# Reading two DRAM bounces in parts, and reordering the first batches, in a spectral-filter and channel-mix kernel

## The chip, the cores and the metric

The kernel runs on one core of a Trainium2 chip. The metric is the device time of one execution in microseconds (us). The kernel before takes 669.4 us (median of four runs, 668.0 to 670.7).

Names: PE is the matrix engine, ACT the scalar engine, DVE the vector engine, POOL the general engine, SP the sync engine, which here only issues DMAs. A line such as L344 is a line of the kernel's source; the same statement has another number in another version.

## The reference, cut to what matters

```python
def _attn_ref(x, w_r, w_i, b_r, b_i):            # x: 8 batches, 3072 positions, 256 channels
    X = np.fft.rfft(x, axis=1)
    Yr = Xr @ w_r - Xi @ w_i + b_r               # complex 256x256 product per frequency
    Yi = Xr @ w_i + Xi @ w_r + b_i
    ... soft threshold with lam = 0.01 ...
    return np.fft.irfft(Y, n=x.shape[1], axis=1)

def _moe_ref(x, mu_k, mu_r, w_k, w_v, w_r):      # x: the result of the above
    x_prev = ... x shifted by one position ...
    k = np.maximum((mu_k * x + (1 - mu_k) * x_prev) @ w_k, 0.0)
    v = k * k @ w_v
    return sigmoid((mu_r * x + (1 - mu_r) * x_prev) @ w_r) * v
```

## The kernel before

The transform of 3072 = 96 x 32 positions is done in two stages with matrix products, and the way back likewise. For each batch b there are three groups of work on PE:

- first(b): 16 products of 512 columns, giving A (96 partitions, by quarters q of the 32 indices n2);
- middle(b): second transform, complex mix, threshold, and second transform back, giving V;
- last(b): first transform back, giving YT, from which the token products (L575, L600, L617) of the batch are made.

Between first and middle, and between middle and last, the data changes its partition axis. This is done by a bounce through DRAM: A goes out to Adr and comes back as A2, V goes out to Vdr and comes back as V2. The two bounces are what the change touches:

```python
# first(b), after the quarter q has been copied out of PSUM
nc.sync.dma_start(out=Adr[b][:, 8 * q:8 * q + 8, :], in_=a)
if q == 3:
    at(k + WRITE_US, fetch)
def fetch(k):                                     # four DMAs, each to 32 partitions, 512-byte runs
    A2[b] = a2_pool.tile([128, NG, D], BF16, name="A2")
    for cj in range(4):
        nc.sync.dma_start(out=A2[b][32 * cj:32 * cj + 32],
                          in_=Adr[b][24 * cj:24 * cj + 24].rearrange("g n d -> n g d"))
    done["A2", b] = k + READ_US                   # what the planner believes
# middle(b), after the unit u (of six) has been copied out of PSUM
for cj in range(4):                               # four stores a unit, 512-byte runs
    nc.sync.dma_start(out=Vdr[b][24*cj + 4*u:24*cj + 4*u + 4].rearrange("g n d -> n g d"),
                      in_=vt[32 * cj:32 * cj + 32])
def fetch(k):                                     # after the sixth: four DMAs to 96 partitions, 4 KB runs
    for q in (2, 3, 0, 1):
        nc.sync.dma_start(out=V2[b, q], in_=Vdr[b][:, 8 * q:8 * q + 8, :])
    done["V2", b] = k + READ_US
```

The order of the instructions on every engine is fixed while the kernel is built, by a planner in Python. It keeps a clock of its own and takes, whenever PE is free by that clock, the unit with the earliest due time whose needs are `done`. Each engine and the SP queue then run that order: at one L501 of the changed kernel PE stood 18.8 us with 16 products behind it (L629) that do not read what it waited for.

```python
READ_US, WRITE_US = 7.0, 5.0
...
fb += first(b, 0.0, 1.0) if b == 0 else first(b, *((45.0, 52.0) if b == 1 else (s - 0.9 * P, s - 0.1 * P)))
fa += middle(b, 20.0, 44.0) if b == 0 else middle(b, s, s + 0.5 * P)
fc += last(b, 55.0, 60.0) if b == 0 else last(b, s + 0.75 * P, s + 0.95 * P)
```

Of the kernel before, what the change touches and what calls it, by code (L numbers as in the profile page):

```python
# [22 lines left out]
def kernel(  # L23
# [31 lines left out]
        return ctx.enter_context(tc.tile_pool(name=name, bufs=bufs))  # L55

    a_pool, a2_pool, xt_pool, xt0_pool = pool("ap", 3), pool("a2p", 2), pool("xtp", 3), pool("xt0p", 1)
    r1_pool, ym_pool, v_pool, v2_pool = pool("r1p", 2), pool("ymp", 3), pool("vp", 3), pool("v2p", 4)
    yt_pool, mx_pool, rl_pool, k2_pool = pool("ytp", 2), pool("mxp", 2), pool("rlp", 3), pool("k2p", 2)
    rg_pool, o_pool = pool("rgp", 3), pool("op", 2)  # L60

# [147 lines left out]


    heap, seq = [], itertools.count()
    free = {"pe": 0.0, "act": 8.0, "dve": 14.0}
    done, slots = {}, {}

    def at(key, fn):
        heapq.heappush(heap, (key, next(seq), fn))
# [53 lines left out]


    Adr, A2, Vdr, V2, YT = {}, {}, {}, {}, {}
    READ_US, WRITE_US = 7.0, 5.0

    def first(b, t0, t1):

        live = {}

        def make(q, p):
            def issue(ps, h, end):  # L280
                if p == 0:
                    if q == 0:
                        Adr[b] = dram.tile([2 * 48, N2, D], BF16, name="Adr")
                    live["A"] = a_pool.tile([96, 8, D], BF16, name="A")
                xt, a = xs[b, q], live["A"]
                for i in range(2):
                    nc.tensor.matmul(ps[:96, 512 * i:512 * i + 512], FT,  # L287
                                     xt[:, 4 * p + 2 * i:4 * p + 2 * i + 2, :], start=True, stop=True)

                def evac(k):  # L290
                    e = copy(k, a[:, 4 * p:4 * p + 4, :], ps[:96].rearrange("p (n d) -> p n d", n=4),
                             1.03, 1.22)
                    release(h, e)
                    if p == 1:
                        at(e, store)

                def store(k):
                    nc.sync.dma_start(out=Adr[b][:, 8 * q:8 * q + 8, :], in_=a)
                    done["a", b, q] = k + WRITE_US
                    n = 4 * b + q + 4  # L300
                    if 8 <= n < 4 * B:
                        load_x(n // 4, n % 4)
                        done["x", n // 4, n % 4] = k + 9.0
                    if q == 3:
                        at(k + WRITE_US, fetch)

                def fetch(k):
                    A2[b] = a2_pool.tile([128, NG, D], BF16, name="A2")
                    for cj in range(4):
                        nc.sync.dma_start(out=A2[b][32 * cj:32 * cj + 32],  # L310
                                          in_=Adr[b][24 * cj:24 * cj + 24].rearrange("g n d -> n g d"))
                    done["A2", b] = k + READ_US
                    if b == 0:

                        nc.gpsimd.tensor_copy(out=junk, in_=A2[0][:, 0, 0:1])
                        load_big()
                        for n in range(4):
                            load_x(1, n)
                            done["x", 1, n] = k + 18.0

                at(end, evac)

            needs = [("x", b, q), "FT"] + [("mid", 0)] * (b == 1)
            if q == 3 and p == 1 and b >= 2:
                needs.append(("mid", b - 2))
            if q == 0 and p == 0 and b >= 2:
                needs.append(("A2", b - 2))
            n = 4 * b + q - 3
            if p == 0 and n >= 0:
                needs.append(("a", n // 4, n % 4))  # L330
            return Unit(t0 + (t1 - t0) * (2 * q + p) / 8, 0.44, needs, issue)

        return [make(q, p) for q in range(4) for p in range(2)]
# [3 lines left out]
    def middle(b, t0, t1):  # L337
# [76 lines left out]
        def back(u):  # L414
            def issue(ps, h, end):
# [2 lines left out]
                    nc.tensor.matmul(ps[:, 256 * i:256 * i + 256], GI[:, 4 * u + i, :],  # L418
                                     y[:, 256 * i:256 * i + 256], start=True, stop=True)
                if u == 0:  # L420
                    Vdr[b] = dram.tile([2 * 48, N2, D], BF16, name="Vdr")
                vt = v_pool.tile([128, 4, D], BF16, name="V")

                def evac(k):
# [2 lines left out]
                    at(e, store)  # L427

                def store(k):
                    for cj in range(4):  # L430
                        nc.sync.dma_start(
                            out=Vdr[b][24 * cj + 4 * u:24 * cj + 4 * u + 4].rearrange("g n d -> n g d"),
                            in_=vt[32 * cj:32 * cj + 32])
                    done["v", b, u] = k + WRITE_US
                    if u == NU - 1:
                        at(k + WRITE_US, fetch)

                def fetch(k):
                    for q in range(4):
                        V2[b, q] = v2_pool.tile([96, 8, D], BF16, name="V2")  # L440
                    for q in (2, 3, 0, 1):
                        nc.sync.dma_start(out=V2[b, q], in_=Vdr[b][:, 8 * q:8 * q + 8, :])
                    done["V2", b] = k + READ_US

                if u == NU - 1:
                    done["mid", b] = end
# [4 lines left out]
        for s in range(NU + 2):  # L451
# [10 lines left out]
            if 0 <= s - 2 < NU:  # L462
                u = s - 2
                needs = [("y", b, u), "GI"]
                if u == NU - 1 and b >= 1:
                    needs.append(("last", b - 1))
                n = 6 * b + u - 3
                if n >= 0:
                    needs.append(("v", n // 6, n % 6))
                units.append(Unit(f + 3 * g, 0.44, needs, back(u)))  # L470
# [4 lines left out]
    def last(b, t0, t1):  # L475
# [3 lines left out]
        def make(n, half, qd):  # L479
            def issue(ps, h, end):  # L480
# [5 lines left out]
                for i in range(4):  # L486
                    n2 = 16 * half + 4 * i + qd
                    for c in range(NCD):
                        nc.tensor.matmul(pv[:, c, :, i, :], V2[b, n2 // 8][:, n2 % 8, 128 * c:128 * c + 128],  # L489
                                         FI, start=True, stop=True)  # L490
                flat = yt.rearrange("p c h z n s -> p (c h) z n s")[:, :, half]

# [157 lines left out]
    def table_gi(n):  # L650
# [17 lines left out]
            at(end, evac)  # L668
        return issue

    def tables(k):
        make_g()
        run_on("act", k, 3.0)
        done["G"] = run_on("dve", free["act"], 0.5)

    P = 74.0
    START = 60.0
    tok, val, fa, fb, fc = [], [], [], [], []
    for b in range(B):
        s = START + P * (b - 1)  # L680
        fb += first(b, 0.0, 1.0) if b == 0 else first(b, *((45.0, 52.0) if b == 1 else (s - 0.9 * P, s - 0.1 * P)))
        fa += middle(b, 20.0, 44.0) if b == 0 else middle(b, s, s + 0.5 * P)
        fc += last(b, 55.0, 60.0) if b == 0 else last(b, s + 0.75 * P, s + 0.95 * P)
    for t in range(NT):
        s = START + P * t / 6
        d = P / 6
# [11 lines left out]
                            [("k2", t, i) for i in range(4)] + [("rg", t)], v_unit(t, p), part=p))  # L698

    for q in range(4):  # L700
        done["x", 0, q] = 5.0 + 3.3 * q
    done["FT"] = 8.0
    at(13.3, tables)
    tab = [Unit(18.0, 0.1, ["FT"], table_fi)]
    tab += [Unit(18.0 + n, 0.5, ["G"], table_gi(n)) for n in range(3)]
    streams = [tok, val, fa, fb, fc, tab]
    at(60.0 - 7.0, lambda k: mix_tokens(0, k))

    place, held, t = [0] * len(streams), {}, 0.0
    while any(n < len(s) for n, s in zip(place, streams)):  # L710
# [52 lines left out]
```

## Time and profile before

| | before |
|---|---|
| time, median | 669.4 us |
| span of the profiled run | 662.8 us |
| PE busy | 593.6 us (90%) |
| first L344 (middle(0) begins) | 31.97 us |
| first token product (L575) | 87.29 us |
| from there to the end | 575.5 us |

PE bounds the kernel from about 100 us on; the start is bound by the two bounces of batch 0, one after the other. The prediction below shows the lines for this. One more view is needed, the windows of the trace while A2 of batch 0 was read and nothing else ran. Columns: stretch, length, busy time of PE, weight loads, DVE, ACT and POOL with the number of instructions, granted PE clock, mean busy share of the 16 DMA engines, GB/s.

```profile
26.00:28.00 2.00, 0.00 (x0) 0.00 (x0) 0.00 (x0) 0.00 (x0) 0.00 (x0) 0.50 1.20 193
28.00:30.00 2.00, 0.00 (x0) 0.00 (x0) 0.00 (x0) 0.00 (x0) 0.00 (x0) 0.50 1.20 177
```

A DMA to 32 partitions in runs of 512 bytes moved about 185 GB/s, with a busy share of 1.20 for the 16 engines (above 1, so it serves here only for comparison).

### The profile page before, as it was taken

How to read it: one execution, taken by the hardware profiler on the slowest of the kernel's cores; microseconds unless marked ns; L12 is line 12 of the kernel's file. 1: busy time of each engine (PE TensorE's matmuls, PEld its weight loads, DVE VectorE, ACT ScalarE, POOL GpSimd, SP SyncE). 2: the span in 40 equal slices, each digit the busy share in tenths (PEclk: the TensorE clock that was granted, in tenths of full speed). 3: DMA queues.
4: the chain of work that ended last, by engine and by line, in shares of the span. 5: the costliest groups of instructions: out<-in, count | busy, mean ns of one | idle time of the engine just before them, and what ended most of it. 6: DMA issues, size and time to landing. Idle time of an engine off the chain costs nothing.

```text
span 662.8 us, 12033 instructions
## 1 busy us (share of the span) xinstructions
PE 593.6 (90%) x4722; PEld 435.5 (66%) x4801; DVE 483.8 (73%) x732; ACT 443.5 (67%) x469; POOL 25.2 (4%) x57
## 2 busy tenths in 40 slices
PE   4295379999999989998999989999999999999996
PEld 1273247777776767765777767766777777777764
DVE  5164368788778877797678787688677896788883
ACT  6254357767777767776577767778687767766662
POOL 5021000000000000000000000000000000000000
PEclk9689579999999999999999999999999999999999
DMA  8697996362247954488155874379233852362223
GB/s 182 119 189 166 290 213 121 79 183 65 57 112 175 230 128 111 103 227 197 33 128 128 237 146 96 88 202 207 86 104 104 223 113 68 78 183 56 65 72 88
DMA packets 75593, 90.33 MB, mean 136 GB/s; under 512 B 8976, under 2 KB 59920, under 8 KB 75536
## 3 DMA queue, kind: packets, MB, share of 16 engines
q1 hardware_dynamic: 69696, 75.53, 44.5%
q0 software_dynamic: 5840, 14.03, 12.5%
q8 instruction: 37, 0.61, 0.4%
q14 instruction: 20, 0.16, 0.1%
HBM read 53.22 MB, written 50.33 MB: 156 GB/s over the span
## 4 chain that ended last, share of the span: by engine, by line
PE 66%; DMA 17%; ACT 6%; DVE 5%; issue 3%; SPq 1%; POOL 0%; DVEq 0%; ACTq 0%; POOLq 0%
PE banks L617 22%; PE banks L575 19%; PE banks L394 11%; DMA Adr<-A 7%; DMA A<-Adr 6%; PE banks L600 4%; ACT rl L581 3%; PE banks L361 3%; PE banks L418 2%; PE banks L383 2%; ACT A L234 2%; PE banks L287 2%; DMA Vdr<-V 1%; DVE V L236 1%; PE banks L489 1%
## 5 line engine op out<-in xcount | busy, mean ns | idle before, releaser
L581 ACT ACTIVATE rl<-banks 128x1024 bf16<-128x1024 f32 x192 | 195.0, 1029 | 86.1 <-PE banks L575 73.2
L575 PE MATMUL banks<-xk,wk 128*128 128x512 bf16 x706 | 191.1, 383 | 4.0 <-DVE xk L553 1.4
L617 PE MATMUL banks<-wv,k 128*128 128x256 bf16 x1536 | 184.5, 274 | 0.4 <-DVE k L587 0.3
L587 DVE TENSOR_TENSOR k<-rl 128x1024 bf16<-128x1024 bf16 x192 | 131.8, 687 | 53.6 <-ACT rl L581 53.5
L617 PEld LDWEIGHTS <-k 128*128 128x128 bf16 x1536 | 150.3, 98 | 30.1 <-issue 1.8
L575 PEld LDWEIGHTS <-wk 128*128 128x128 bf16 x768 | 73.4, 98 | 57.9 <-issue 4.3
L394 PEld LDWEIGHTS <-XT 128*128 128x128 bf16 x768 | 75.4, 98 | 23.9 <-issue 0.8
L402 ACT ACTIVATE r<-banks,neglam 128x1024 bf16<-128x1024 f32 x48 | 53.4, 1113 | 40.6 <-PE banks L394 39.4
L406 DVE SCALAR_TENSOR_TENSOR Y<-banks,r 128x1024 bf16<-128x1024 f32 x48 | 58.5, 1222 | 28.1 <-ACT r L402 28.0
L394 PE MATMUL banks<-wr,XT 128*128 128x256 bf16 x384 | 73.8, 274 | 0.9
L394 PE MATMUL banks<-wi,XT 128*128 128x256 bf16 x384 | 73.8, 274 | 0.0
L553 DVE SCALAR_TENSOR_TENSOR xk<-diff,muk,YT 128x512 bf16<-128x512 bf16 x96 | 70.0, 746 | 0.6
L553 DVE SCALAR_TENSOR_TENSOR xr<-diff,mur,YT 128x512 bf16<-128x512 bf16 x96 | 69.2, 745 | 0.0
L624 DVE TENSOR_TENSOR o<-banks,rg 128x1024 f32<-128x1024 f32 x48 | 58.5, 1218 | 7.7 <-PE banks L617 7.7
L234 ACT ACTIVATE XT<-banks 128x1024 bf16<-128x1024 f32 (+2 forms) x39 | 37.8, 970 | 35.4 <-PE banks L361 23.5
L234 ACT ACTIVATE A<-banks 96x1024 bf16<-96x1024 f32 x49 | 49.2, 1020 | 17.6 <-DMA Adr<-A 12.0
L287 PE MATMUL banks<-xs,FT 96*96 96x512 bf16 x128 | 39.5, 420 | 19.0 <-ACT A L234 11.7
L600 PE MATMUL banks<-wrm,xr 128*128 128x256 bf16 x384 | 49.8, 272 | 3.5 <-ACT rl L581 2.2
L234 ACT ACTIVATE YT<-banks 128x768 bf16<-128x768 f32 x51 | 39.9, 815 | 16.2 <-PE banks L489 16.2
L605 ACT ACTIVATE rg<-banks 128x1024 bf16<-128x1024 f32 x48 | 49.2, 1026 | 1.9 <-PE banks L600 1.9
L600 PEld LDWEIGHTS <-xr 128*128 128x128 bf16 x384 | 37.1, 97 | 14.1 <-issue 3.8
L234 ACT ACTIVATE V<-banks 128x1024 bf16<-128x1024 f32 x33 | 33.8, 1023 | 9.9 <-PE banks L418 8.1
(91 smaller groups left out, 401.8 us busy)
## 6 DMA issues: line engine op xcount, KB each, us to landing
out_dram<-o SPq DMA_DIRECT2D x192, 128.0 KB, 2.2
xs<-in_x_dram POOLq DMA_DIRECT2D x32, 384.0 KB, 8.1
Adr<-A SPq DMA_DIRECT2D x32, 384.0 KB, 6.6
A<-Adr SPq DMA_DIRECT2D x32, 384.0 KB, 6.6
Vdr<-V SPq DMA_DIRECT2D x192, 64.0 KB, 1.8
V<-Vdr SPq DMA_DIRECT2D x32, 384.0 KB, 6.2
wk<-in_moe_w_k_dram POOLq DMA_DIRECT2D x1, 512.0 KB, 5.4
wv<-in_moe_w_v_dram POOLq DMA_DIRECT2D x1, 512.0 KB, 8.4
```

Of the source, the lines that this page charges most:

```text
L234: nc.scalar.activation(out, in_, AF.Copy, bias=0.0, scale=1.0)
L287: nc.tensor.matmul(ps[:96, 512 * i:512 * i + 512], FT, xt[:, 4 * p + 2 * i:4 * p + 2 * i + 2, :], start=True, stop=True)
L394: nc.tensor.matmul(o, lhs, w[:, c, :], start=False, stop=(w is wi and c == NCD - 1 and (i == 1 or not (u or half))))
L402: nc.scalar.activation(r1, ps, AF.Relu, bias=neglam, scale=1.0)
L406: nc.vector.scalar_tensor_tensor(out=y, in0=ps, scalar=LAM, in1=r1, op0=ALU.add, op1=ALU.min)
L553: nc.vector.scalar_tensor_tensor(out=m[:, c, :], in0=df[:, c, :], scalar=mu[:, c:c + 1], in1=yp[:, c, :], op0=ALU.mult, op1=ALU.add)
L575: nc.tensor.matmul(ps[:, 512 * f:512 * f + 512], wk[:, c, 128 * ff:128 * ff + 128], xk[:, c, :], start=(c == 0), stop=(c == NCD - 1))
L581: nc.scalar.activation(rl, ps, AF.Relu, bias=0.0, scale=1.0)
L587: nc.vector.tensor_tensor(out=k2, in0=rl, in1=rl, op=ALU.mult)
L600: nc.tensor.matmul(ps[:, 256 * q:256 * q + 256], xr[:, c, 128 * q:128 * q + 128], wrm[:, c, :], start=(c == 0), stop=(c == NCD - 1))
L617: nc.tensor.matmul(ps[:, 256 * q:256 * q + 256], K2[t][:, ff, 128 * q:128 * q + 128], wv[:, ff, :], start=(ff == 0), stop=(ff == NCF - 1))
L624: nc.vector.tensor_tensor(out=o.rearrange("p q d -> p (q d)"), in0=ps, in1=rg, op=ALU.mult)
```

## The change

Its intent: shorten the way from the first transform to the second, and from the second to the last, by reading each bounce in parts while the rest is still computed; use fewer and longer store DMAs for V; keep batch 1 out of batch 0's way; and keep the PE clock up with 24 products that nobody reads.

```diff
-    READ_US, WRITE_US = 7.0, 5.0
+    READ_US, WRITE_US = 6.0, 5.0
@@ first: fetch A2 in quarters for batch 0, in halves for the others
-                    if q == 3:
-                        at(k + WRITE_US, fetch)
+                    if b == 0:
+                        at(land, lambda k: fetch(k, q, 1))
+                    elif q % 2:
+                        at(land, lambda k: fetch(k, q - 1, 2))
...
-                        nc.sync.dma_start(out=A2[b][32 * cj:32 * cj + 32],
-                                          in_=Adr[b][24 * cj:24 * cj + 24].rearrange("g n d -> n g d"))
+                        sl = slice(8 * q0, 8 * (q0 + nq))
+                        nc.sync.dma_start(out=A2[b][32 * cj + 8 * q0:32 * cj + 8 * (q0 + nq)],
+                                          in_=Adr[b][24 * cj:24 * cj + 24, sl].rearrange("g n d -> n g d"))
@@ first(1) after last(0), not after middle(0)
-            needs = [("x", b, q), "FT"] + [("mid", 0)] * (b == 1)
+            needs = [("x", b, q), "FT"] + [("last", 0)] * (b == 1)
@@ middle: one store a unit; V2 read after unit 3 (16 groups) and after unit 5 (8 groups)
-                    Vdr[b] = dram.tile([2 * 48, N2, D], BF16, name="Vdr")
+                    Vdr[b] = dram.tile([128, NG, D], BF16, name="Vdr")
...
+                    nc.sync.dma_start(out=Vdr[b][:, 4 * u:4 * u + 4, :], in_=vt)
+                    if u == 3:
+                        at(land, lambda k: fetch(k, 0, 16))
+                    elif u == NU - 1:
+                        at(land, lambda k: fetch(k, 16, 8))
...
                     for cj in range(4):
+                        r0 = 24 * cj + g0
                         nc.sync.dma_start(
-                            out=Vdr[b][24 * cj + 4 * u:24 * cj + 4 * u + 4].rearrange("g n d -> n g d"),
-                            in_=vt[32 * cj:32 * cj + 32])
+                            out=V2[b][r0:r0 + ng],
+                            in_=Vdr[b][32 * cj:32 * cj + 32, g0:g0 + ng].rearrange("n g d -> g n d"))
@@ later first transforms end 0.1 of a period earlier; 2 x 12 unread products
-    ... (s - 0.9 * P, s - 0.1 * P) ...
+    ... first(b, s - 0.9 * P, s - 0.2 * P)
+    tab += [Unit(19.0, 2.6, [("A2p", 0, 1)], spin(lambda: A2[0][0:16, 0, 0:128], lambda: A2[0][0:16, 1:3, :])),
+            Unit(44.0, 2.6, [("V2p", 0, 0), ("mid", 0)], spin(lambda: V2[0][0:16, ...], ...))]
```

Left out: needs that follow from the buffers, and planner numbers of the start (START 60 to 50, landing of batch 0's pieces 3 us).

More of the change, by code (lines that the diff above doesn't have):

```diff
@@ L57 @@
     a_pool, a2_pool, xt_pool, xt0_pool = pool("ap", 3), pool("a2p", 2), pool("xtp", 3), pool("xt0p", 1)
-    r1_pool, ym_pool, v_pool, v2_pool = pool("r1p", 2), pool("ymp", 3), pool("vp", 3), pool("v2p", 4)
+    r1_pool, ym_pool, v_pool, v2_pool = pool("r1p", 2), pool("ymp", 3), pool("vp", 3), pool("v2p", 1)
     yt_pool, mx_pool, rl_pool, k2_pool = pool("ytp", 2), pool("mxp", 2), pool("rlp", 3), pool("k2p", 2)
@@ L211 @@
     heap, seq = [], itertools.count()
-    free = {"pe": 0.0, "act": 8.0, "dve": 14.0}
+    free = {"pe": 0.0, "act": 6.0, "dve": 13.3}
     done, slots = {}, {}
@@ L298, in store @@
                     nc.sync.dma_start(out=Adr[b][:, 8 * q:8 * q + 8, :], in_=a)
-                    done["a", b, q] = k + WRITE_US
+                    land = k + (3.0 if b == 0 else WRITE_US)
+                    done["a", b, q] = land
                     n = 4 * b + q + 4
@@ L303, in store, with fetch @@
                         done["x", n // 4, n % 4] = k + 9.0
-                    if q == 3:
-                        at(k + WRITE_US, fetch)
-                def fetch(k):
-                    A2[b] = a2_pool.tile([128, NG, D], BF16, name="A2")
-                    for cj in range(4):
-                        nc.sync.dma_start(out=A2[b][32 * cj:32 * cj + 32],
-                                          in_=Adr[b][24 * cj:24 * cj + 24].rearrange("g n d -> n g d"))
-                    done["A2", b] = k + READ_US
-                    if b == 0:
-                        nc.gpsimd.tensor_copy(out=junk, in_=A2[0][:, 0, 0:1])
-                        load_big()
-                        for n in range(4):
-                            load_x(1, n)
-                            done["x", 1, n] = k + 18.0
+                    if b == 0:
+                        at(land, lambda k: fetch(k, q, 1))
+                    elif q % 2:
+                        at(land, lambda k: fetch(k, q - 1, 2))
+                def fetch(k, q0, nq):
+                    if q0 == 0:
+                        A2[b] = a2_pool.tile([128, NG, D], BF16, name="A2")
+                    for cj in range(4):
+                        sl = slice(8 * q0, 8 * (q0 + nq))
+                        nc.sync.dma_start(out=A2[b][32 * cj + 8 * q0:32 * cj + 8 * (q0 + nq)],
+                                          in_=Adr[b][24 * cj:24 * cj + 24, sl].rearrange("g n d -> n g d"))
+                    done["A2p", b, q0] = k + (3.0 if b == 0 else READ_US)
+                    if q0 + nq == 4:
+                        done["A2", b] = done["A2p", b, q0]
+                        if b == 0:
+                            nc.gpsimd.tensor_copy(out=junk, in_=A2[0][:, 0, 0:1])
+                            load_big()
+                            for n in range(4):
+                                load_x(1, n)
+                                done["x", 1, n] = k + 20.0
                 at(end, evac)
-            needs = [("x", b, q), "FT"] + [("mid", 0)] * (b == 1)
-            if q == 3 and p == 1 and b >= 2:
+            needs = [("x", b, q), "FT"] + [("last", 0)] * (b == 1)
+            if q == 0 and p == 0 and b >= 2:
                 needs.append(("mid", b - 2))
@@ L429, in store, with fetch @@
                 def store(k):
+                    nc.sync.dma_start(out=Vdr[b][:, 4 * u:4 * u + 4, :], in_=vt)
+                    land = k + (3.0 if b == 0 else WRITE_US)
+                    done["v", b, u] = land
+                    if u == 3:
+                        at(land, lambda k: fetch(k, 0, 16))
+                    elif u == NU - 1:
+                        at(land, lambda k: fetch(k, 16, 8))
+                def fetch(k, g0, ng):
+                    if g0 == 0:
+                        V2[b] = v2_pool.tile([96, N2, D], BF16, name="V2")
                     for cj in range(4):
+                        r0 = 24 * cj + g0
                         nc.sync.dma_start(
-                            out=Vdr[b][24 * cj + 4 * u:24 * cj + 4 * u + 4].rearrange("g n d -> n g d"),
-                            in_=vt[32 * cj:32 * cj + 32])
-                    done["v", b, u] = k + WRITE_US
-                    if u == NU - 1:
-                        at(k + WRITE_US, fetch)
-                def fetch(k):
-                    for q in range(4):
-                        V2[b, q] = v2_pool.tile([96, 8, D], BF16, name="V2")
-                    for q in (2, 3, 0, 1):
-                        nc.sync.dma_start(out=V2[b, q], in_=Vdr[b][:, 8 * q:8 * q + 8, :])
-                    done["V2", b] = k + READ_US
+                            out=V2[b][r0:r0 + ng],
+                            in_=Vdr[b][32 * cj:32 * cj + 32, g0:g0 + ng].rearrange("n g d -> g n d"))
+                    done["V2p", b, g0] = k + (3.0 if b == 0 else READ_US)
+                    if g0 + ng == NG:
+                        done["V2", b] = done["V2p", b, g0]
                 if u == NU - 1:
@@ L464, in middle @@
                 needs = [("y", b, u), "GI"]
-                if u == NU - 1 and b >= 1:
+                if u == 0 and b >= 1:
                     needs.append(("last", b - 1))
@@ L488, in issue @@
                     for c in range(NCD):
-                        nc.tensor.matmul(pv[:, c, :, i, :], V2[b, n2 // 8][:, n2 % 8, 128 * c:128 * c + 128],
+                        nc.tensor.matmul(pv[:, c, :, i, :], V2[b][:, n2, 128 * c:128 * c + 128],
                                          FI, start=True, stop=True)
@@ L669, in table_gi, with spin, issue @@
         return issue
+    def spin(lhs, rhs):
+        def issue(ps, h, end):
+            for _ in range(12):
+                nc.tensor.matmul(ps[:, 0:512], lhs(), rhs(), start=True, stop=True)
+            release(h, end + 0.2)
+        return issue
     def tables(k):
@@ L676 @@
     P = 74.0
-    START = 60.0
+    START = 50.0
     tok, val, fa, fb, fc = [], [], [], [], []
@@ L680 @@
         s = START + P * (b - 1)
-        fb += first(b, 0.0, 1.0) if b == 0 else first(b, *((45.0, 52.0) if b == 1 else (s - 0.9 * P, s - 0.1 * P)))
-        fa += middle(b, 20.0, 44.0) if b == 0 else middle(b, s, s + 0.5 * P)
-        fc += last(b, 55.0, 60.0) if b == 0 else last(b, s + 0.75 * P, s + 0.95 * P)
+        if b == 0:
+            fb += first(b, 0.0, 1.0)
+            fa += middle(b, 20.0, 44.0)
+            fc += last(b, 45.0, 50.0)
+        else:
+            fb += first(b, START, START + 1.0) if b == 1 else first(b, s - 0.9 * P, s - 0.2 * P)
+            fa += middle(b, s + (0.2 * P if b == 1 else 0.0), s + 0.5 * P)
+            fc += last(b, s + 0.75 * P, s + 0.95 * P)
     for t in range(NT):
@@ L700 @@
     for q in range(4):
-        done["x", 0, q] = 5.0 + 3.3 * q
-    done["FT"] = 8.0
-    at(13.3, tables)
+        done["x", 0, q] = 6.0 + 2.8 * q
+    done["FT"] = 5.0
+    at(16.0, tables)
     tab = [Unit(18.0, 0.1, ["FT"], table_fi)]
     tab += [Unit(18.0 + n, 0.5, ["G"], table_gi(n)) for n in range(3)]
+    tab += [Unit(19.0, 2.6, [("A2p", 0, 1)], spin(lambda: A2[0][0:16, 0, 0:128], lambda: A2[0][0:16, 1:3, :])),
+            Unit(44.0, 2.6, [("V2p", 0, 0), ("mid", 0)],
+                 spin(lambda: V2[0][0:16, 0, 0:128], lambda: V2[0][0:16, 1:3, :]))]
     streams = [tok, val, fa, fb, fc, tab]
-    at(60.0 - 7.0, lambda k: mix_tokens(0, k))
+    at(START - 7.0, lambda k: mix_tokens(0, k))
     place, held, t = [0] * len(streams), {}, 0.0
```

## The prediction

> **What bounds the kernel now.** I read the slices of the page first, then the windows table, then the chain of waits and the timeline of the first 90 us, and last the waits of TensorE (PE) after 88 us. The slices:
>
> ```profile
> PE   4295379999999989998999989999999999999996
> ...
> PEclk9689579999999999999999999999999999999999
> ```
>
> One slice is 16.6 us. From the seventh on PE is busy nine tenths or more, so the kernel is bound by PE there, and only removed PE idle counts. The first six slices are different. The windows table (columns: stretch, length, PE, weight loads, DVE, ACT and POOL busy, then granted clock, DMA share, GB/s):
>
> ```profile
> 20.00:30.00 10.00, 0.00 (x0) 0.00 (x0) 0.00 (x0) 0.72 (x1) 0.00 (x0) 0.65 0.90 164
> 30.00:40.00 10.00, 7.98 (x59) 6.15 (x61) 3.53 (x5) 2.52 (x3) 5.20 (x9) 0.66 0.80 117
> ...
> 60.00:70.00 10.00, 1.29 (x6) 0.55 (x5) 0.52 (x1) 0.22 (x1) 1.01 (x2) 0.70 1.07 218
> 70.00:80.00 10.00, 3.43 (x17) 1.49 (x17) 3.66 (x3) 3.87 (x4) 0.51 (x1) 0.50 1.01 329
> ```
>
> There are two holes: at 20 to 32 us batch 0 waits for its first bounce, at 57 to 80 us for its second. The chain of waits names what fills them (start, length, what):
>
> ```profile
> 18.48 2.98 DMA Adr<-A
> ...
> 23.06 8.78 DMA A<-Adr
> ...
> 42.39 6.81 DMA Vdr<-V
> ...
> 60.30 11.49 DMA Adr<-A
> ...
> 73.20 8.43 DMA Adr<-A
> ...
> 83.54 8.54 DMA A<-Adr
> ```
>
> And the timeline shows when each stage begins:
>
> ```profile
> 31.97 0.59 PE L344 MATMUL banks<-G,A 128*128 128x256 f16 x2 [12.44 <-DMA A<-Adr]
> ...
> 60.30 1.44 SPq L298 DMA_DIRECT2D Adr<-A  x3
> 71.16 1.95 SPq L442 DMA_DIRECT2D V<-Vdr  x4
> ...
> 79.94 4.34 PE L489 MATMUL banks<-FI,V 96*128 96x96 f16 x52 [0.37 <-DMA V<-Vdr]
> ...
> 87.29 0.38 PE L575 MATMUL banks<-xk,wk 128*128 128x512 bf16 x1 [1.11 <-DVE xk L553]
> ```
>
> The second hole matters most. Middle(0) (second transform, mix, transform back) ends on PE at 56.4. Its last V stores leave at 60.2, because each unit needs four store issues, and the batch 1 stores of A, with five x loads from POOL, go out at once. The read of V waits until 71.2, is whole near 80, and the first token product starts at 87.3. From there to 662.8 are 575.5 us, nearly all PE work. The steady part has one PE wait worth naming (us, times, longest):
>
> ```profile
> PE banks L344 <- DMA A<-Adr: 11.1, 4, 3.4
> ```
>
> This is each new batch waiting for A2. 3.4 of it is batch 1; 7.7 comes later, and a colder clock after one of them (0.82 to 0.84 over 310 to 320 us) costs about 1.5 more.
>
> [...] clock 0.50 from 24 to 34 us, 1.00 from 38. [...] the sync queue waits 55.2 us for Adr<-A before L310.
>
> **The change part by part.**
>
> *Batch 0's first bounce in quarters.* Before: the last A store leaves at 18.48, lands 2.98 later, four reads are issued at 21.6 to 23.1, and all is there at 31.9. The last A eviction sat behind the G table activations (13.7 to 16.7) and the G0 copies; by the planner's keys it now goes ahead of them, but on DVE it still waits for the bsel work that ends near 16.3, so the store leaves about 17.6, 0.8 us earlier, and lands near 20.6. The read of 1.57 MB ran at 230 GB/s just after its start and at 177 to 193 afterwards. A quarter is 0.39 MB. On 16 engines the last quarter would take some 2 us of transfer after 2 us of issue: ready at 25 to 26. On 8 engines, at a rate per engine between those two (11 to 14 GB/s), the four quarters need 14 to 18 us in all from about 13 us on, beside the later stores: ready at 27 to 31. I take 28, so 4 us gained.
>
> *24 unread products.* Each is 512 columns, 0.216 us at full clock (eight L575 take 1.73), so 12 take 2.6, or 5.2 at half. The first 12 follow the 24 table products, which will end near 21, and end by 26: inside the wait. They spare the half clock that middle(0) had up to about 36 us, about 2 us. The second 12 lie in the second hole and likewise spare last(0) its 0.50 (80 to 84 us). On the path their cost is about 0.
>
> *V store by one DMA per unit.* 192 issues become 48. In middle(0), DVE and ACT waited 2.4 and 1.65 us for V buffers; these go. Middle(0) took 24.4 us; less 2 for clock, and partly less the buffer waits (they overlap each other, and the last back product still waits for relu and shrink): 23. It ends on PE at 51, and its last V lands after 1 us eviction and 3 of store, at 55.
>
> *V read in two parts, first(1) moved after last(0).* The first 16 groups are read under middle(0). The last 8 (0.52 MB, 8 engines) take 2 us of issue, 4 to 5 of transfer, part of it beside the issue: 6, so 61. No A stores or x loads of batch 1 stand in front any more, which saves the 60.3 to 71.2 wait. From V2 whole to the first token product it was 87.3 - 79.9 = 7.4, with A evictions of batch 1 and 2 in between and PE at half clock; now 5.5. First token product: about 66.5 instead of 87.3, so 21 earlier.
>
> *What moves behind it.* By 87.3 the old kernel had done first(1) and first(2), 32 products of 512 columns, 7 us; most of this now falls after the first token product: +7. A2 of batch 1 comes late: last(0)'s end, plus about 6 for eviction, 8 for stores beside x loads, 6 to 7 for the half read, so 20 us into the tokens, where the planner expects about 16. PE can stand there for some 4 us, and tokens with first(1) and first(2) alone need as much of ACT and DVE as of PE. The old kernel lost about 6 between 85 and 100 (PE 2.3 and 2.9 of 5, then a clock of 0.63 to 0.68). I call this even.
>
> *Steady batches.* First(b) ends 0.1 of 74, so 7.4 us, earlier, and the last read is half as long. The waits for A2 of 1 to 3 us should go: -8 with their clock.
>
> Sum: 66.5 + 575.5 + 7 - 8 = 641 against 662.8. The ratio 0.967 applied to 670.37 gives 648.
>
> **Rivals.**
> 1. The quarters on 8 engines are as slow as the old whole read. For: [...] a share of 1.2 at 181 GB/s in the old read[...]. Against: the same read began at 230. Then everything starts 3 to 4 us later: 652; with a slow V tail as well, 656.
> 2. The gain is given back: PE stops at middle(1) since A2(1) cannot come before 86. For: old A stores took 8 to 11 us beside x loads, the planner counts 5. Against: six token tiles of 8 us PE work each are there to be done, if the order lets them. A stall of 10 would make 655 to 658.
> 3. Bytes and engines allow more: quarters use 16 engines and the V tail lands within 4: first token product at 61 to 62, time 642.
> 4. The sync queue blocks: it waits in order, and split reads wait twice a batch for stores that take longer than planned, which delays output stores and, by the two o buffers, PE. Against: PE is 95% busy with such waits today (55.2 us), and the V stores take 144 issues off. At worst +5.
>
> **Range and chances.** The uncertain terms are the engine limit (±4), the V tail (±2), the stall at middle(1) (±5) and the steady gain (±3); as independent terms that is about 7 to 8, and the runs of before differ by 0.4%. So 638 to 659. The limit of 2% faster is 657, more than one such deviation above 648: 0.86. Slower by 2% would need the saving of 20 us to be overturned: 0.01.
>
> **What would show it right or wrong.** L344 first at 28 (not 32), with clock near 1.00; L442 in two groups, the second issued near 55; first L575 at 62 to 70; the stretch from it to the end 572 to 580 us; L344's later waits below 3 us in all. I am wrong if the first L344 stays at 31 or later, if PE stands over 6 us at middle(1), or if steady batches show new waits of PE for V2 or for PSUM.

## The result

The changed kernel takes 811.3 us (median of four runs, 809.0 to 816.5): slower by a fifth, ratio 1.2132, 95% interval 1.2065 to 1.2198. Ratios here are the mean time of one kernel's fast runs over that of the other's in the same rounds, so they need not be quite the ratio of the medians.

The slices of the page after (one slice is 20.4 us):

```profile
PE   4366383975999199973999469991999669994996
...
PEclk9997596996999689995999869996999969997999
```

PE is no longer busy throughout. Every fourth or fifth slice has a hole, one for each batch, and the clock falls with it. The timeline of the start:

```profile
47.21 0.59 PE L351 MATMUL banks<-G,A 128*128 128x256 f16 x2 [14.57 <-DMA A<-Adr]
...
75.02 5.30 PE L687 MATMUL banks<-V 16*128 16x512 bf16 x12 [4.67 <-DMA V<-Vdr]
94.55 5.28 PE L501 MATMUL banks<-FI,V 96*128 96x96 f16 x64 [14.23 <-DMA V<-Vdr]
...
104.29 0.38 PE L587 MATMUL banks<-xk,wk 128*128 128x512 bf16 x1 [0.73 <-DVE xk L565]
```

Middle(0) begins at 47.2 us instead of 32.0, and the first token product at 104.3 instead of 87.3: 17 us later. From there to the end are 710.1 us instead of 575.5: 134.6 more. The waits of PE (us in all, times, longest) say where those are:

```profile
PE banks L501 <- DMA out_dram<-o: 91.5, 6, 18.8
...
PE banks L501 <- issue: 19.3, 1, 19.3
PE banks L351 <- DMA A<-Adr: 14.6, 1, 14.6
PE banks L501 <- DMA V<-Vdr: 14.2, 1, 14.2
...
PE banks L351 <- DMA Adr<-A: 12.4, 1, 12.4
```

L501 is last(b), which needs V2. The profile names the DMA whose semaphore moved last, here an output store; but an L501 product reads nothing but V2 and FI, and the second read of V2 is what had just been issued. Without batch 0's wait (14.2) these are 110.8 us in seven batches, 16 a batch. With the 12.4 at batch 1's L351 and the 7 us of first(1) and first(2) that moved behind the first token product, and less the 11.1 of waits for A2 that the kernel before had in this stretch, that is 119 of the 134.6. Most of the rest is clock: PE is busy 618.2 us instead of 593.6, 10.6 of it in the unread products, 14 with the same products at a lower clock after each hole (mean granted clock 0.900 in the profiled run, 0.965 before).

One change of batch in the chain of waits (start, length, what), on the SP queue and on PE:

```profile
450.36 13.96 DMA Vdr<-V
...
464.40 0.29 SPq L450
...
466.37 8.99 DMA out_dram<-o
475.37 0.80 PE banks L501 x8
```

```profile
440.40 2.11 SPq L450 DMA_DIRECT2D V<-Vdr  x4
442.56 6.01 SPq L315 DMA_DIRECT2D A<-Adr  x4
448.67 2.27 SPq L437 DMA_DIRECT2D Vdr<-V  x2
451.03 0.62 SPq L298 DMA_DIRECT2D Adr<-A  x1
464.40 1.49 SPq L450 DMA_DIRECT2D V<-Vdr  x4
```

```profile
455.57 1.03 PE L587 MATMUL banks<-xk,wk 128*128 128x512 bf16 x4
475.37 0.80 PE L501 MATMUL banks<-FI,V 96*128 96x96 f16 x8 [18.77 <-DMA out_dram<-o]
475.97 3.62 PE L629 MATMUL banks<-wv,k 128*128 128x256 bf16 x16
```

The first part of V2 is issued at 440.4, half of the next A2 right behind it, then the last two V stores. The last store lands 14 us after its issue, with both reads in front of it in the queue; only then is the second part issued (464.4), and V2 is whole 11 us later. PE has come to last(b) at 456.6 and stands to 475.4. The 16 products behind it take 3.62 us instead of 1.91; the granted clock was 0.50 from 476 to 480 us.

Why are the reads so slow? The windows of four stretches in which one kind of read runs nearly alone: a quarter of A2 (8 partitions a DMA), half of A2 (16), the first part of V2 (16), the second (8).

```profile
36.00:39.00 3.00, 0.00 (x0) 0.00 (x0) 0.00 (x0) 0.00 (x0) 0.00 (x0) 1.00 0.65 54
```

```profile
116.00:118.00 2.00, 1.95 (x15) 1.40 (x15) 1.94 (x4) 1.86 (x2) 0.51 (x1) 1.00 1.26 97
```

```profile
72.00:74.00 2.00, 0.00 (x0) 0.00 (x0) 0.00 (x0) 0.00 (x0) 0.00 (x0) 0.50 1.23 100
...
86.00:88.00 2.00, 0.00 (x0) 0.00 (x0) 0.00 (x0) 0.00 (x0) 0.00 (x0) 0.50 0.64 58
```

All four have runs of 512 bytes, as the read of A2 before had. With 32 destination partitions it made 185 GB/s, with 16 it makes 97 to 100, with 8 it makes 54 to 58. The share of busy engines is the same for 32 and 16 partitions (1.2) and half for 8 (0.65): the 8 engines that the prediction assumed for 8 partitions fit the step from 16 to 8 in the share, but not the step from 32 to 16 in the rate, where the share is the same (1.20 and 1.23) and the rate about half (185 and 100 GB/s).

The theory for this, **theory P**: the partitions to which a read goes set its rate. Rows on few neighbouring partitions are slow, and the same rows set apart will be faster. The first half is what the trace shows: 185, 100 and 54 to 58 GB/s for 32, 16 and 8 neighbouring partitions. The second was a supposition when e2 and e4 were written; the rates expected there, about 180 and 100 GB/s, are estimates and amount to 16 rows set apart going like the 32 neighbours before, and 8 like 16 neighbours. The rivals: the number of engines and the run length set the rate (**E**); the loss is the V store standing behind the first read (**Q**); the new order is at fault, not the transfers (**O**).

### The profile page after: what moved, and what is told of

Read it like the earlier page. It is cut to its first block, busy times and chain, and to the rows that moved or that the text cites. A ratio compares the mean times of both kernels' runs of the same rounds, so it can differ in the third digit from the quotient of the medians.

```text
span 814.4 us, 11982 instructions
## 1 busy us (share of the span) xinstructions
PE 618.2 (76%) x4746; PEld 446.5 (55%) x4825; DVE 491.5 (60%) x739; ACT 435.9 (54%) x462; POOL 25.2 (3%) x57
## 3 DMA queue, kind: packets, MB, share of 16 engines
q0 software_dynamic: 5840, 14.03, 10.6%
## 4 chain that ended last, share of the span: by engine, by line
PE 54%; DMA 28%; ACT 6%; DVE 4%; SPq 4%; issue 3%; ACTq 0%; DVEq 0%; POOLq 0%
PE banks L629 17%; PE banks L587 14%; DMA Vdr<-V 12%; PE banks L401 9%; DMA out_dram<-o 6%; DMA Adr<-A 5%; DMA V<-Vdr 4%; PE banks L612 3%; PE banks L501 3%; ACT rl L593 3%; PE banks L368 2%; PE banks L425 2%; PE banks L390 2%; SPq L450 2%; DMA A<-Adr 2%
## 5 line engine op out<-in xcount | busy, mean ns | idle before, releaser
L587 PE MATMUL banks<-xk,wk 128*128 128x512 bf16 x707 | 193.5, 384 | 4.7 <-issue 1.1
L629 PE MATMUL banks<-wv,k 128*128 128x256 bf16 x1536 | 194.7, 283 | 2.2 <-ACT rg L617 1.5
L629 PEld LDWEIGHTS <-k 128*128 128x128 bf16 x1536 | 154.9, 101 | 37.9 <-issue 3.7
L501 PE MATMUL banks<-FI,V 96*128 96x96 f16 x512 | 34.7, 224 | 126.0 <-DMA out_dram<-o 91.5
L501 PEld LDWEIGHTS <-V 96*128 96x128 bf16 x512 | 30.8, 108 | 136.1 <-DMA out_dram<-o 50.3
L515 DVE COPY YT<-YT 128x576 bf16<-128x576 bf16 x16 | 4.9, 309 | 103.2 <-ACT YT L234 103.2
L234 ACT ACTIVATE A<-banks 96x1024 bf16<-96x1024 f32 x43 | 42.9, 1018 | 10.4 <-PE banks L287 9.1
```

Source lines behind the costliest of these rows:

```text
L234: nc.scalar.activation(out, in_, AF.Copy, bias=0.0, scale=1.0)
L501: nc.tensor.matmul(pv[:, c, :, i, :], V2[b][:, n2, 128 * c:128 * c + 128], FI, start=True, stop=True)
L587: nc.tensor.matmul(ps[:, 512 * f:512 * f + 512], wk[:, c, 128 * ff:128 * ff + 128], xk[:, c, :], start=(c == 0), stop=(c == NCD - 1))
L629: nc.tensor.matmul(ps[:, 256 * q:256 * q + 256], K2[t][:, ff, 128 * q:128 * q + 128], wv[:, ff, :], start=(ff == 0), stop=(ff == NCF - 1))
```

## The experiments

The labels are in the order in which they ran. e1 to e4 ran on one chip, e5 to e8, e9 to e12 and e13 to e15 each likewise; the kernel before took 668.0, 668.8, 669.7 and 670.4 us beside them. All fifteen results were correct, and all runs in the fast state but the longest of e7 (705.5 us).

### e1_v_old: the second bounce as before

```diff
-   nc.sync.dma_start(out=Vdr[b][:, 4 * u:4 * u + 4, :], in_=vt)     # and two reads, 16 and 8 groups
+   for cj in range(4): nc.sync.dma_start(out=Vdr[b][24*cj+4*u:24*cj+4*u+4].rearrange("g n d -> n g d"), ...)
+   for q in (2, 3, 0, 1): nc.sync.dma_start(out=V2[b, q], in_=Vdr[b][:, 8 * q:8 * q + 8, :])
```

> The changed kernel with the second bounce (layout of Vdr, four stores a unit, one read as four DMAs of 96 partitions) as before, and without the second group of 12 unread products; all else as changed. Theory P (the reads of V and A in parts are slow [...]: 32 partitions 185 GB/s, 16 partitions 100, 8 partitions 56 in the trace): the 20 us PE wait at L501 of every batch goes, the slow first start (L351 at 47 us) stays; about 660 us, between 650 and 680. Rival O (the loss comes from the new order, first(1) after last(0) and the earlier first(b), not from the bounce): stays above 750 us.

Measured: 705.6 us. The holes of 16 us a batch are gone, so O in its form (above 750) falls, and most of the loss lies in the second bounce: 106 of 142 us. But the figure expected was missed by 25 us at least. Middle(0) still began late, at 41.1 us (6 us before the changed kernel's, with the same reads of A; why is not known), batch 1's middle stood 13.6 us at L351, and PE still waited 33.3 us in 17 pieces for V2, behind the halves of A2 in the queue.

### e2_v_spread: the same reads of V, rows four partitions apart

```diff
-   out=V2[b][r0:r0 + ng]                           # r0 = 24 * cj + g0
+   out=V2[b][4 * g0 + cj : 4 * (g0 + ng) + cj - 3 : 4]
+   # FI's rows in the same order: FTP = FT with its columns (c g) as (g c)
```

> The changed kernel with the rows of V2 put at partition 4g+cj instead of 24cj+g (FI's rows permuted to match): the same DMAs, the same 512-byte runs, the same counts of 16 and 8 destination partitions, but 4 apart. Theory P: part 1 goes [...] from 100 to about 180 GB/s, part 2 [...] from 57 to 100 GB/s or more; the wait per batch at L501 falls from 20 us to about 10; total 720 to 760 us. Rival E (number of DMA engines and the 512-byte runs set the rate): both rates stay, 811 us.

Measured: 745.4 us, 66 us less. The rates of the two parts in the windows:

```profile
72.00:74.00 2.00, 0.00 (x0) 0.00 (x0) 0.00 (x0) 0.00 (x0) 0.00 (x0) 0.50 1.25 182
...
78.00:80.00 2.00, 2.00 (x6) 0.67 (x5) 0.00 (x0) 0.00 (x0) 0.00 (x0) 0.50 0.44 131
```

The first part went from 100 to 182 GB/s at the same busy share, the second from 58 to 131 at a lower one. Numbers of DMAs and of partitions, bytes, run length and source addresses are as before; only the place of the rows in SBUF is other. E falls. L503 began at 82.7 us instead of 94.6 in batch 0.

### e3_v_end: both parts read after the last store

```diff
-   if u == 3: at(land, lambda k: fetch(k, 0, 16))
-   elif u == NU - 1: at(land, lambda k: fetch(k, 16, 8))
+   if u == NU - 1:
+       at(land, lambda k: fetch(k, 0, 16))
+       at(land, lambda k: fetch(k, 16, 8))
```

> The changed kernel with both parts of V read after the last V store has landed. Rival Q (the loss is that the last V store queues behind part 1 of the read: 10 to 14 us to landing instead of 3): the V stores land in about 3 us and the total falls by 10 us a batch, to about 735. Theory P: the same 1.57 MB at 100 and 57 GB/s lie on the path all the same, about 19 us after the store: 800 to 830 us.

Measured: 817.9 us; last(0) began at 94.2 us against 94.6. So Q falls as the cause: with the last store in front of both reads nothing is won, because the same two slow reads then come after it. That the store waits behind a read is seen in the trace (14 us to landing at 450 us above), but it only hands on the time of that read.

### e4_a_spread: A2's rows two apart

```diff
-   out=A2[b][32 * cj + 8 * q0 : 32 * cj + 8 * (q0 + nq)]
+   lo = 32 * cj + 16 * (q0 % 2) + q0 // 2          # row n2 at partition 2 * (n2 % 16) + n2 // 16
+   out=A2[b][lo : lo + 16 * nq - 1 : 2]
+   # the first unread group reads row 0 only; n2c, the index for G, permuted; last reads V2[b][:, 2 * (n2 % 16) + n2 // 16]
```

> The changed kernel with row n2 of the second transform at partition 2(n2 mod 16)+n2/16 of its block of 32 (the G tables' index and the order of last's products permuted to match): the quarters' 8 and the halves' 16 destination partitions lie 2 apart. Theory P: quarters go [...] 56 to about 100 GB/s, so L351 starts near 33 us instead of 47; the halves from 100 to about 180 GB/s, which also shortens the queue in front of the V store by some 4 us a batch; total 760 to 790 us. Rival E: L351 stays at 47 us and the total at 811.

Measured: 768.2 us, 43 less, and middle(0) at 33.6 us instead of 47.2. A quarter alone in the window:

```profile
29.00:31.00 2.00, 0.00 (x0) 0.00 (x0) 0.00 (x0) 0.00 (x0) 0.00 (x0) 1.00 0.60 111
```

From 54 to 111 GB/s at 8 partitions and about the same share of engines (0.60, and 0.65 before): the place of the rows alone doubled the rate.

### e5_both_spread

The edits of e2 and e4 together.

> The changed kernel with both spreads, that of e2 (V2 rows 4 apart) and that of e4 (A2 rows 2 apart). Theory P: the two gains of 66 and 43 us lie mostly at different places and add: about 700 us (690 to 720), with L351 first near 33 us and some 5 us of wait at L501 a batch left. If [...] one of the two edits had changed the order by luck, they would not add: 740 us or more.

Measured: 700.9 us (697.1 and 704.7). The two gains, 66 and 43, add to 110. Middle(0) begins at 32.7, the first token product at 79.1 us. So with this planner the slow reads cost about 110 of 142 us. Waits of up to 7.4 us a batch for V2 remained: V2 still came later than the planner had been told.

### e6_order_only: all bounces as before, only the order changed

The V bounce as in e1; A read in one piece for every batch; no unread products.

```diff
-   if b == 0: at(land, lambda k: fetch(k, q, 1))
-   elif q % 2: at(land, lambda k: fetch(k, q - 1, 2))
+   q == 3 and at(land, lambda k: fetch(k, 0, 4))
```

> The changed kernel with both bounces read as before (V in the old layout with four stores a unit and one whole read, A in one whole read of 32 partitions per DMA for every batch) and without the unread products: what is left of the change is the order (first(1) after last(0), the first transforms of later batches ending 7.4 us earlier, the planner's numbers). By the prediction's steps for order alone: about 655 us. Theory S (moving first(1) behind last(0) makes PE stand for A2 of batch 1, 12 us in the changed kernel, and gives back what it gains): 665 to 680 us with a wait of 10 us or more at the second L351.

Measured: 673.5 us (671.6 to 675.1), ratio 1.0056 (1.0010 to 1.0102). The first token product came at 77.4 us, 10 earlier than in the kernel before, and nothing was won. The wait at the second L351 was 3.5 us, not 10, so theory S's mechanism missed though its time was right. The stretch behind the first token product grew by 20 us, to 595.9: 7.6 us are new waits for V2 (of 19.5 in all; the other 11.9 lie at batch 0, before it) and about 7 the work moved; the rest was not traced.

### e7_spread_halves and e8_spread_early

Both have V as before, A2's rows two apart and every A2 read in halves; e8 has first(1) before last(0).

```diff
+   (e7) V as in e1, A2 rows as in e4, q % 2 and at(land, lambda k: fetch(k, q - 1, 2)) for every b
-   (e8) needs = ... [("last", 0)] * (b == 1);   first(b, START, START + 1.0);   middle(1) from s + 0.2 * P
+   (e8) needs = ... [("mid", 0)] * (b == 1);    first(b, 44.0, 45.0);           middle(1) from s
```

> V's bounce as before, A2's rows 2 apart, every A read in two halves (batch 0 too), first unread group kept, first(1) after last(0). Theory P: halves at 180 GB/s, L351 first near 30 us, first token product near 78, a wait at batch 1's L351 below 10 us and no L351 waits later: about 655 us (645 to 668).

> As e7, but the first transform of batch 1 before last(0), right after middle(0), as in the kernel before. If moving it is a net loss (theory S) this beats e7 by 5 us or more; if it is a net gain, it loses by 5 or more. Estimate 650 us.

Measured: 696.6 us (692.9 to 705.5) and 689.6 us (684.1 to 693.4). Both expectations missed by 30 us and more. The start was as expected (middle(0) at 29.6 and 29.5 us), and after batch 1 (3.4 us in both) no wait for A2 was left. But PE waited 42.2 and 40.9 us for V2 (12.3 and 20.0 of it at batch 0), twice as long as in e6. In one batch the last V store of e7 left at 300.9 us and V2 was whole at 316.4: 15.5 us where the planner counts 11. Why e6, with the same numbers, waits only half as long is not settled.

### e9_plan: the planner is told what the reads take

```diff
-   done["A2p", b, q0] = k + (3.0 if b == 0 else READ_US)
+   done["A2p", b, q0] = k + (8.0 if b == 0 else 13.0)
-   done["V2p", b, g0] = k + (3.0 if b == 0 else READ_US)
+   done["V2p", b, g0] = k + (15.0 if b == 0 else 21.0)
```

> The changed kernel with one thing altered: the planner, which fixes the order of each engine when the kernel is built, is told what the reads took on the chip: V2 ready 21 us after the second read's place (15 for batch 0) instead of 6 (3), A2 13 us (8) instead of 6 (3). All transfers stay as slow as they were. Theory H (the slow read costs 20 us a batch because PE, which runs its instructions in the fixed order, reaches last(b) too early and stands, while token products that could have run lie behind it): the waits at L501 fall from 20 us to below 5 a batch, the late start stays; total about 700 us (680 to 725). Rival D (the data is needed at that time whatever the order): 790 us or more.

Measured: 733.5 us, 78 less than the changed kernel with every read as slow as there. Rival D falls: most of each wait was only an order that came too early, with token products behind it that could have run. The range expected was missed by 8 us. The wait for V2 at L501 is gone from PE but for batch 0 (13.5 us); in its place stand one of 14.5 us at batch 2's L351, which needs A2, visible as an empty window, and a new wait on DVE that reaches PE:

```profile
190.00:200.00 10.00, 0.00 (x0) 0.00 (x0) 1.62 (x2) 0.00 (x0) 0.00 (x0) 0.50 0.97 196
```

```profile
DVE o L636 <- DMA out_dram<-o: 40.0, 8, 10.2
...
PE banks L287 <- DVE o L636: 17.2, 2, 9.5
...
PE banks L501 <- DVE o L636: 7.0, 2, 5.0
```

DVE cannot write the next output tile because the stores of the one before stand on the SP queue, behind reads (four of them at 188.6 us behind a read of A2 whose issue took from 181.1 to 188.4), and PE stood 24.2 us for it. This is the prediction's fourth rival; of all the runs only e9 shows it.

### e10_order_plan: e6 with truer numbers

```diff
-   READ_US, WRITE_US = 6.0, 5.0
+   READ_US, WRITE_US = 11.0, 6.0
```

> e6 (order alone, both bounces as before) with the planner told 11 us for a read and 6 for a write instead of 6 and 5. Theory H: the waits of e6 at L496 (23 us) and later L351 shrink to a third, the early first token product (77 us) stays: about 655 us (645 to 665), faster than e6's 673 and than the kernel before. Rival D: 673.

Measured: 668.3 us (667.3 to 669.2), ratio 0.9984 (0.9955 to 1.0014). The waits for V2 fell from 19.5 to 11.3 us, all of it at batch 0; those for A2 rose from 19.5 to 24.4 (9.6 of it at batch 0). So with the bounces as before, order and numbers together win nothing clear; the expectation of 655 missed.

### e11_plan_spread: both mended

The edits of e5, and V2 at 12 us (8 for batch 0), A2 at 10 (6) in the planner.

> e5 (both spreads) with the planner told 12 us for V2 (8 for batch 0) and 10 for A2 (6). Theories P and H together: first L351 near 33 us, first token product near 80, waits at L501 below 3 us a batch: about 660 us (648 to 675), against 701 of e5.

Measured: 655.9 us (653.4 to 660.1), ratio 0.9805 (0.9759 to 0.9851): 155 us below the changed kernel and 14 below the kernel before. Faster is clear; whether by 2% is not, as the interval holds 0.98. The slices of its page:

```profile
PE   4594879997999999999999999999999999999996
...
PEclk9997799998999999999999999999999999999999
```

From the sixth slice on (81 us) PE is busy nearly throughout, and the holes at every batch are gone.

### e12_no_spin: the changed kernel without the unread products

```diff
-   tab += [Unit(19.0, 2.6, [("A2p", 0, 1)], spin(...)), Unit(44.0, 2.6, [("V2p", 0, 0), ("mid", 0)], spin(...))]
```

> The changed kernel without the 24 unread products. The prediction's step (they lie in waits and cost nothing on the path; the first group keeps the clock up): within 4 us of the changed kernel's 811, if anything 1 to 2 us longer from a colder clock at middle(0). A rival, that they hold PE when the data arrives: 2 to 5 us shorter.

Measured: 809.2 us (808.3 to 810.2) against 811.3. The intervals of the two ratios to the kernel before overlap (1.2057 to 1.2132 and 1.2065 to 1.2198), so they cost or win nothing that can be told from zero. The run does not decide between the step and its rival: 2.1 us shorter lies in the range of both.

### e13, e14, e15: what the other parts are worth once the reads are mended

Each is e11 with one edit: e13 has first(1) before last(0) (the edit of e8), e14 reads V in one part (below), e15 has no unread products (the edit of e12).

```diff
+   (e14) if u == NU - 1: at(land, lambda k: fetch(k, 0, 24))
```

> e11 (both spreads, planner told the measured times) with the first transform of batch 1 back in its old place, before last(0). The prediction's step: its stores and x loads then lie in front of the read of V, so the first token product comes some 8 to 10 us later than e11's 78 us, and the total is 5 us longer or more (660 or more). Rival S (first(1) late only moves 7 us of work behind the first token product and makes A2 of batch 1 late): within 3 us of e11's 656 or below.

> e11 with V read in one part of 24 rows a DMA after the last store, rows 4 apart[...]; without the second unread group. If reading in two parts is worth something by itself, the first token product of e11 comes earlier by about 4 us and the total is 3 to 6 us shorter than here (660 here). If what matters is only that the planner's times hold, the totals agree within 2 us.

> e11 without the 24 unread products. In e11 the second group held PE for some us (wait of 6.3 us in front of it and products at the half clock), the read being short now. If they cost: 2 to 4 us shorter than e11 (653). If they pay by the clock: 1 to 3 us longer.

Measured, against e11's 655.9 and ratio 0.9805:

| | median us | ratio to before, 95% interval | first token product |
|---|---|---|---|
| e13 first(1) early | 657.9 | 0.9833 (0.9792 to 0.9874) | 91.6 us |
| e14 V in one read | 654.7 | 0.9785 (0.9734 to 0.9836) | 79.0 us |
| e15 no unread products | 658.0 | 0.9822 (0.9803 to 0.9842) | 78.3 us |

None differs clearly from e11; the intervals leave room for some 6 us. e13 is the instructive one: its first token product comes 14 us later, and the median is only 2 us longer. The traces show part of the reason: by 91.6 us PE had been busy for 43.5 us without the unread products, against 49.7 in e11, so it was some 6 us of busy time behind and not 14. (The trace of e13 is of the slowest of its four runs, 663.1 us.)

In e14 the read of 24 rows, four apart, ran at 196 to 206 GB/s with a share of 0.92, three quarters of the 1.23 above, so with less engine time than the 16 neighbouring rows of the changed kernel took for 100. That speaks against E once more. It also shows how far spreading went: with 24 rows instead of the 16 of e2's first part, four apart in both, the rate rose only from 182 to about 200. What limits it there was not tried.

None of these three parts of the change is worth anything that these runs can show; what e11 wins over the kernel before comes with spread reads (182 GB/s for 16 rows of V in e2), with an order that matches them, and with one store a unit for V. These were not tried one at a time on the kernel before.

## Why the prediction was wrong

The prediction was 648 us, range 638 to 659, 0.86 for faster; the result was 811 us.

**The step that failed: the transfer times of the parts.** The prediction took for a quarter of A2 "On 16 engines the last quarter would take some 2 us of transfer" or, on 8 engines, a rate per engine as in the read before; for the last 8 groups of V "4 to 5 of transfer"; and the 16 groups "are read under middle(0)" at no cost. Measured: the quarters made 54 GB/s where 11 to 14 GB/s on each of 8 engines, 88 to 112, was counted, so A2 was whole at 47 us instead of 28; the last part of V took about 9 us (0.52 MB at 58 GB/s); the 16 groups took over 10 us (1.05 MB at 100 GB/s) and held up the store behind them. Of the two limits in theory P and its rival E, the place of the rows in SBUF and the engines, the prediction had weighed only the engines; their number, 8 for 8 partitions, was an assumption. Spreading the rows about doubled the rates, from 100 to 182 and from 58 to 131 GB/s in e2 and from 54 to 111 in e4, with the DMAs and their counts of rows unchanged. The prediction's first rival was of this kind, but its size, 652 to 656, was far off.

**The second: what a late V2 does in the steady batches.** The prediction looked for V's read only at batch 0 and let the later batches gain 8 us. There the order is fixed by a planner that was told 6 us. A read that takes over 20 us from the last store's issue, as at 450 to 475 us above, makes PE stand in every batch. e9 shows that 78 us of the loss disappear when only the planner's numbers are altered. (These and the 110 of e5 are not to be added: both take away the same waits at L501.) The prediction's closing line named it as a way to be wrong ("steady batches show new waits of PE for V2") without a number.

**What held.**

- *Waits for A2 in the later batches go.* In the changed kernel L351 waits on PE only at batch 0 and batch 1, but there PE stands at L501 in every batch, so this alone shows little. e11, without those stands, has no wait for A2 after batch 0 either (5.1 us there).
- *Middle(0) takes 23 us.* From 47.2 to 70.4 it took 23.2. But the 2 us counted for the clock are not shown: e12, without the unread products and with a recorded 0.50 from 32 to 49.5 us, took the same 23.2. The figure was in part luck.
- *PE can stand at middle(1) (rival 2).* It did, 12.4 us at 123 to 135 us, where the prediction called the stretch even.
- *The sync queue blocks (rival 4).* Seen in e9 only, 40.0 us on DVE and 24.2 of PE behind it; in the changed kernel PE does not wait for it.
- *The stretch after the first token product.* Predicted 575.5 + 7 - 8 = 574.5. With the reads and numbers mended (e11) it is 653.3 - 77.6 = 575.7. The sum of the steady part fits a kernel whose reads come when the planner expects them; its terms (+7, -8) were not measured one by one, so part of this may be luck. The start was not, even there: 77.6 instead of 66.5, as A2 was whole at 31.9 and V2 at 68.8 us, and from V2 to the first token product it took 8.8 us, not 5.5.
- *The unread products cost nothing on the path*, by e12 (809.2 us without them, 811.3 with). That they spare the half clock was the author's estimate, and wrong: in the changed kernel last(0) began 14 us after the second group and ran its 64 products in 5.28 us at a clock of 0.50, as slow as before; and the first products of middle(0) took 0.59 us for two, as before and as in e12 without the unread products, although the clock is recorded as 1.00 there and over the wait of 14.6 us in front of them. Nor was the long gap the reason: in e11 last(0) began 1.7 us after the second group and still took 5.28 us.

**What the prediction measured by.** It counted a microsecond at the first token product as one of the total. e6 and e13 against e11 show that this does not hold: 10 us earlier brought nothing, 14 us later cost nothing clear. What counts is how much PE has stood idle, and that is not read from which product comes first.

**What stays open.** Why e7 and e8 waited twice as long for V2 as e6; how much of e11's gain over the kernel before is the rates, how much the order and how much the single store a unit; why the first read of A took 6 us less in e1; and what makes the reads into neighbouring partitions slow: the runs show the rates of rows next to each other, two apart and four apart, and no cause behind them.

## What to carry to other kernels

Before a transfer is cut into parts, ask which partitions a part lands on: parts of 8 or 16 neighbouring partitions ran at 0.3 and 0.5 of the rate of 32 here (54 to 58 and 97 to 100 GB/s of 185), and putting the rows two or four apart brought them to 0.6 to 1.0 of it (111 to 182 GB/s), at the price of a permuted table. When the order of instructions is fixed ahead, the transfer times that the plan assumes are as much a part of the kernel as the transfers; measure them after each change, for here PE, held to the fixed order, paid for an optimistic number in every batch (some 16 us). And count the idle time of the bounding engine, not the time at which a favourite stage begins.
